# Seven half-size products for the output matmul, and other runs for the strided heads' loads

## The chip, the cores and the metric

One NeuronCore of a Trainium2 chip. The metric is the device time of one execution in microseconds (us). TensorE multiplies and writes PSUM; VectorE and ScalarE read PSUM and work element by element; GpSimd (POOL) works on SBUF alone; SyncE (SP) issues the transfers between HBM and SBUF in the order of its queue.

## The reference

```python
def reference(**kwargs):
    attn_out = _attn_ref(q, k, v)          # 4 batches, 8 heads, 576 tokens, 64 wide
    x = attn_out.transpose(0, 2, 1, 3).reshape(2304, 512)
    x = _moe_ref(x, w_in, w_out, g_ln)     # 512 -> 1024 -> h*softmax(h), normalised -> 512
    a, b = x @ w_a, x @ w_b                # 512 -> 1536
    return (a * b @ w_out2).astype(np.float32)   # 1536 -> 512
```

Heads 0 to 3 attend to the last 32 tokens, heads 4 to 7 to the tokens whose distance is a multiple of 32. The weights are float64.

## The kernel before, in words

Products are made from 16-bit halves: each operand is split into a high part (ScalarE) and a remainder (VectorE), and a product is three matmul passes, high-high, high-low and low-high (`PASSES`).

The first stage runs attention batch by batch. A group is two heads. `load_qk` loads q and k of a group, for strided heads as runs of two tokens (512 bytes) on 96 partitions; `group_T` transposes them on TensorE, six transposes of 96 columns, and ScalarE evicts them into an order by residue (L661). The tiles of batch 0 (`direct`) write their scaled probabilities into a zeroed buffer `pfb` that holds one of the two `lnT` buffers. `moe1` and `s2` are the first two dense layers and follow the batches; their results go to HBM as `y_scr`.

The second stage is three passes (`ps`) over three blocks of 768 tokens (`n`). Pass `ps` covers two of six weight columns (`u`). For a block and a `u`, `ab` calls `product` twice, for x @ w_a and x @ w_b. `product` already uses seven half-size products in place of eight (14 tiles of 6 matmuls of 384 columns a `u`, L1332): operands are A11 to S4 of the weights, from `split_ab`, and B11 to T4 of y, from `y_load`, and the partial sums are carried from bank to bank by ScalarE copies (L1339). `ab` multiplies the two results (L1381) and splits the product into `p` (L1382, L1384). `out_tile` then multiplies `p` of both `u` with the output weights `wo`, 12 matmuls of 512 columns a tile of 128 tokens (L1397), six tiles a block. In pass one ScalarE scales the result (L1407); in passes two and three VectorE adds it to the partial sums of the pass before (L1404), loaded from `o_scr` into `op`. A block's six tiles come right behind its two `ab`.

`y_load` brings a block of y into `yst` (one buffer, L1221), normalises it and makes its seven operands (L1279, L1284). `conv_ab` and `conv_o` convert the weights of the next pass beside the products; `conv_o` stages in the `wo` buffer itself, of which there are two. The weights of a and b have four buffers by `u`.

PSUM in the second stage: five banks `M` for the products, two `o` for the output, one `Q` for small things. Buffers come from rings; the user of a ring's slot waits for all users of the slot's last buffer, and no buffer is started before the one ahead of it in its ring.

The order of the work is a planner's (`Plan.schedule`): every operation has a cost and a key, a list scheduler orders each engine by key, and 200 passes with noise from a seeded generator look for the order with the shortest modelled time. The emitted program keeps that order on each engine.

Of the kernel before, what the change touches and what calls it, by code (L numbers as in the profile page):

```python
# [10 lines left out]
F32 = mybir.dt.float32  # L11
# [22 lines left out]
NM = S // QT  # L34
QB = 64
# [19 lines left out]
PARAM = dict(back=12, first=40, early=(0,), seed=6, noise=0.1, direct=(0,), stay=0.0, pf1=(),  # L55
             pf2=(), ph1=(), pv=(), pp=(8,), ps1=(), ps2=(), ps3=False, ps4=False, passes=200, e=3,
# [272 lines left out]
def tile_banded_attention_solu_bilinear(  # L329
# [86 lines left out]
    rsqs = const.tile([128, NTT], F32, name="rsqs")  # L416
    zmo = const.tile([128, NP, NCH // NP + 1], F32, name="zmo")
# [4 lines left out]

    for tag, shape, dt in (("rawq", [QT, NM, 2, D], F32), ("rawk", [QT, NM, 2, D], F32)):
        ring("at", tag, shape, dt, pm["raw"])
# [6 lines left out]
    ring("at", "e", [128, 4 * KB], F32, pm["e"])  # L431
# [9 lines left out]
    ring("conv", "sq2", [128, 512], BF16, 2)  # L441
# [36 lines left out]
    def constants_d():  # L478
        nc.gpsimd.memset(mone, -1.0)
        nc.gpsimd.memset(ones_sq, 1.0)  # L480
        nc.gpsimd.memset(onesb, 1.0)
        nc.gpsimd.memset(units, 1.0)
        nc.gpsimd.memset(units[:, 0, 1:2], 1.0 / PSCALE)
        nc.gpsimd.memset(units[:, 1, 1:2], 1.0 / LSCALE)
# [7 lines left out]
    if pm["direct"]:  # L492
# [7 lines left out]
    def from_f64(src, cols, dst=None, dtok=(), fr="f64f", need=(), ps=False):  # L500
# [11 lines left out]
        else:  # L512
            dve(0.5, lambda: nc.vector.tensor_scalar(raw()[:, :, 0], raw()[:, :, 0], 29, None,
                                                     op0=ALU.logical_shift_right), (), (raw,))
        g = f if dst is None else dst if callable(dst) else lambda: dst
# [24 lines left out]
    def load_wout(c):  # L540
        fo = wout_f32(c)
        f = from_f64(w_out[128 * c:128 * c + 128, :], False, fo, (("wof", c),), ps=c in pm["ps2"])
        act(0.9, lambda: nc.scalar.activation(f(), fo, AF.Abs, scale=g_sb[:, c:c + 1], accum_out=wam[:, c:c + 1]),
            ("g", ("wof", c)), (f, ("wam", c)))

    def pow2_scale(am, toks, n, unit, dst, dtok, top=14, least=60, ps="scp", sm=""):


        tp = rings[ps].new()
# [46 lines left out]

    def load_qk(g):
        h0 = 2 * g.pr
        g.raw = [rings[t].new() for t in ("rawq", "rawk")]
        for c, src in ((0, q), (1, k)):  # L600
            t = g.raw[c]
            if g.strided:
                dma(lambda t=t, src=src: nc.sync.dma_start(
                    out=t().rearrange("p i j d -> p i (j d)"),
                    in_=src[g.b, h0:h0 + 2].rearrange("h (i p j) d -> p (h i) (j d)", p=QT, j=2)),
                    (), ((t, 0), (t, 1)), 294912)
                continue
            for h in range(2):
                dma(lambda t=t, h=h, src=src: nc.sync.dma_start(
                    out=t()[:, :, h], in_=src[g.b, h0 + h].rearrange("(m p) d -> p m d", p=QT)),  # L610
# [33 lines left out]
    def group_T(g):  # L644
        g.T = rings["qkT"].new()
        for c in range(2):
# [3 lines left out]
            def transposes(tp=tp, raw=raw):  # L650
                for m in range(NM):
                    i, o = divmod(m, NM // 2)
                    nc.tensor.transpose(tp()[:, i, QT * o:QT * o + QT], raw()[:, m].rearrange("p h d -> p (h d)"),  # L653
                                        ident[:QT, :QT])
            pe(NM * 0.085, transposes, ((raw, 0), (raw, 1), "ident"), (tp,), NM * 144)

            def evac(c=c, tp=tp):
                src = tp()[:, :, :S // 2]
                dst, sc = g.T()[:, c], 1.0 if c else D ** -0.5
                if g.strided:  # L660
                    nc.scalar.activation(dst.rearrange("p (h a t) -> p h a t", h=2, t=NR),  # L661
                                         src.rearrange("p h (t a) -> p h a t", t=NR), AF.Copy, scale=sc)
                else:
                    nc.scalar.activation(dst.rearrange("p (i t) -> p i t", i=2), src, AF.Copy, scale=sc)
            act(1.2 if g.strided else 0.66, evac, (tp,), ((g.T, c),))
# [33 lines left out]

    def att_tile(g, j, fine):  # L700
# [3 lines left out]
        direct = g.b in pm["direct"]  # L704
# [48 lines left out]
        el = ng * nk * 1.25e-3  # L753

        def ev():
            return e()[:, :ng * nk].rearrange("p (c k) -> p c k", c=ng)
# [11 lines left out]
        else:  # L768
            dve(0.07 + el, lambda: nc.vector.tensor_tensor(
                ev().rearrange("p (f c) k -> p f c k", c=npb), sv(),  # L770
                mv().unsqueeze(3).to_broadcast([128, len(banks), npb, nk]), op=ALU.add), (*spt, mx), (e,))
# [5 lines left out]
        dve(0.08, lambda: nc.vector.tensor_scalar(s4()[:, :ng], s4()[:, :ng], u, 1e-9 * u, op0=ALU.mult, op1=ALU.add), (), ss)  # L777
# [5 lines left out]
        if direct:  # L783
            early = g.b in pm["early"]
            pt = rings["y"].new() if early else sp
            tok = (pfb, i % 4)

            def pf():
                return pfb().rearrange("p a f t -> p (a f t)").bitcast(F32)[:, 512 * (i % 4):512 * (i % 4) + ng * W]

            def blocks(t):
# [705 lines left out]
```

## Time and profile before

| | us |
|---|---|
| median of 3 timed runs (lowest to highest) | 712.41 (712.12 to 713.53) |
| the profiled execution | 714.81 |
| its span, first to last instruction | 712.7 |
| TensorE, VectorE, ScalarE, GpSimd busy | 684.6, 494.1, 404.1, 150.5 |

The profile belongs to one execution. Busy time is given by engine, by stretch of the span, and by groups of instructions (line, engine, operation, output and input). The chain that ended last follows the end of the program back to what released each step. "Clock" is the TensorE clock that was granted, as a share of full speed. Overlapping instructions of one engine are counted once in a stretch, and with their whole length in a group's mean.

### The profile page before, as it was taken

What the parts mean: (1) busy time and instruction counts of PE and PEld (TensorE: products, weight loads), DVE (VectorE), ACT (ScalarE), POOL (GpSimd) and SP (SyncE); (2) the same over time, 40 slices, a digit from 0 to 9 for tenths busy, and PEclk for the clock granted to TensorE, in tenths of its full rate; (3) what the DMA queues carried; (4) which work ended last, traced back from release to release, by engine and by line L of the source; (5) the groups of instructions that cost most, each with busy time, mean ns of one, the idle gap of its engine ahead of it and who ended that gap; (6) DMA issues with size and microseconds to landing.
All of it is one profiled execution on the core that took longest, in us unless ns stands there. A gap on an engine that the chain in (4) does not pass through costs nothing.

```text
span 712.7 us, 14218 instructions
## 1 busy us (share of the span) xinstructions
PE 684.6 (96%) x5492; PEld 452.6 (64%) x5492; DVE 494.1 (69%) x1011; ACT 404.1 (57%) x766; POOL 150.5 (21%) x266
## 2 busy tenths in 40 slices
PE   6886899999999999989999999999999999999997
PEld 5674687887887888866555555555555555465553
DVE  5889888677889747987999986656477534434352
ACT  3778677777788646856777585633354423132230
POOL 4554437544656722310000000000000000000000
PEclk9967699999999999999999999999999999999999
DMA  9988979999999946567363253345205043602304
GB/s 182 239 227 206 181 160 186 227 202 221 218 197 246 218 95 169 127 201 255 121 230 101 80 173 132 104 142 179 87 30 178 1 148 88 226 20 77 101 15 162
DMA packets 159327, 109.61 MB, mean 154 GB/s; under 512 B 103702, under 2 KB 137500, under 8 KB 159260
## 3 DMA queue, kind: packets, MB, share of 16 engines
q1 hardware_dynamic: 159260, 108.71, 59.1%
q8 instruction: 43, 0.70, 0.4%
q14 instruction: 24, 0.20, 0.1%
HBM read 65.42 MB, written 27.53 MB: 130 GB/s over the span
## 4 chain that ended last, share of the span: by engine, by line
PE 80%; DVE 6%; DMA 6%; ACT 2%; POOL 2%; issue 2%; SPq 0%; DVEq 0%; ACTq 0%; POOLq 0%
PE M L1332 33%; PE o L1397 19%; PE h L901 12%; PE y L955 11%; DMA raw<-in_moe_w_in_dram 3%; PE s L653 1%; DMA lnT<-ln 1%; PE s L744 1%; DMA PT<-P 1%; PE xbank L848 1%; DMA rawk<-in_k_dram 1%; POOL P L830 1%; DVE wk L916 1%; DVE st L906 1%; DVE y L1279 1%
## 5 line engine op out<-in xcount | busy, mean ns | idle before, releaser
L1332 PE MATMUL M<-y,w 128*128 128x384 f16 x1512 | 255.6, 326 | 0.1
L1332 PEld LDWEIGHTS <-w 128*128 128x128 f16 x1512 | 147.8, 98 | 100.9 <-issue 0.5
L1397 PE MATMUL o<-wo,p 128*128 128x512 f16 x648 | 147.4, 379 | 0.0
L1397 PEld LDWEIGHTS <-p 128*128 128x128 f16 x648 | 63.3, 98 | 71.3
L955 PE MATMUL y<-lnT,wout 128*128 128x256 f16 x864 | 102.5, 276 | 3.5 <-DMA lnT<-ln 3.4
L955 PEld LDWEIGHTS <-wout 128*128 128x128 f16 x864 | 83.2, 99 | 17.6 <-issue 6.6
L901 PE MATMUL h<-win,xh 128*128 128x512 f32 x288 | 81.5, 424 | 1.9 <-DVE wk L916 1.9
L1339 ACT COPY M<-M 128x384 f32<-128x384 f32 x72 | 33.5, 466 | 64.4 <-PE M L1332 64.3
L901 PEld LDWEIGHTS h<-win,xh 128*128 128x128 f32 x288 | 55.5, 201 | 14.3 <-DVE wk L916 1.4
L1404 DVE SCALAR_TENSOR_TENSOR ob<-o,osc,op 128x512 f32<-128x512 f32 x36 | 27.0, 751 | 44.3 <-PE o L1397 43.3
L1382 ACT ACTIVATE p<-A 128x384 f16<-128x384 f32 x72 | 36.8, 521 | 31.5 <-DVE A L1381 31.4
L1384 DVE SCALAR_TENSOR_TENSOR p<-A,p 128x384 f16<-128x384 f32 x72 | 39.0, 553 | 11.1 <-ACT p L1382 10.8
L1381 DVE TENSOR_TENSOR A<-A,M 128x384 f32<-128x384 f32 x36 | 19.9, 553 | 37.6 <-PE M L1332 37.4
L507 ACT ACTIVATE f64f<-raw 128x512 f32<-128x512 f32 x52 | 34.7, 673 | 14.3 <-DMA raw<-in_moe_w_in_dram 6.1
L1343 DVE TENSOR_TENSOR A<-M,V 128x384 f32<-128x384 f32 x36 | 19.9, 555 | 32.2 <-PE M L1332 32.2
L1354 ACT COPY V<-M 128x384 f32<-128x384 f32 x36 | 17.1, 475 | 43.0 <-PE M L1332 42.9
L901 PE MATMUL h<-win,xl 128*128 128x512 f32 x144 | 40.8, 406 | 0.0
L830 POOL TENSOR_TENSOR P<-e,P 128x324 f16<-128x324 f32 (+2 forms) x30 | 32.0, 1072 | 14.5 <-ACT P L829 14.4
L822 POOL TENSOR_TENSOR e<-e,r 128x324 f32<-128x324 f32 (+2 forms) x30 | 26.9, 902 | 33.1 <-DVE r L778 24.2
L901 PEld LDWEIGHTS h<-win,xl 128*128 128x128 f32 x144 | 26.9, 193 | 5.6
L906 DVE TENSOR_REDUCE st<-h 128x1 f32<-128x1024 f32 x18 | 21.9, 1218 | 11.0 <-PE h L901 10.9
L916 DVE SCALAR_TENSOR_TENSOR wk<-h,st,wk 128x1024 f32<-128x1024 f32 x18 | 23.1, 1281 | 9.2 <-POOL st L914 7.4
(173 smaller groups left out, 1051.0 us busy)
## 6 DMA issues: line engine op xcount, KB each, us to landing
raw<-in_moe_w_out_dram SPq DMA_DIRECT2D x20, 512.0 KB
o_scr<-ob SPq DMA_DIRECT2D x36, 256.0 KB
op<-o_scr SPq DMA_DIRECT2D x36, 256.0 KB
raw<-in_moe_w_a_dram SPq DMA_DIRECT2D x12, 512.0 KB
raw<-in_moe_w_b_dram SPq DMA_DIRECT2D x12, 512.0 KB
y_scr<-y SPq DMA_DIRECT2D x14, 384.0 KB
y<-y_scr SPq DMA_DIRECT2D x14, 384.0 KB
y_scr<-ys SPq DMA_DIRECT2D x18, 256.0 KB
```

The costliest lines, as they stand in the source:

```text
L507: act(0.67, lambda: nc.scalar.activation(f(), raw()[:, :, 1].bitcast(F32), AF.Prelu, scale=2.0 ** -112, alpha=-2.0 ** 32), (raw,), (f,))
L830: pool(0.15 + 1.4 * pl, lambda: nc.gpsimd.tensor_tensor(plo, ev(), ph, op=ALU.subtract), (e, ("P2", pi, 0)), (("P2", pi, 1),))
L901: nc.tensor.matmul(h()[:, 512 * n:512 * n + 512], xs[xa]()[:, kk], win[wa][:, kk, 512 * n:512 * n + 512], start=(pi == 0 and kk == 0), sto ...
L906: dve(1.22, lambda: nc.vector.tensor_reduce(st()[:, 0:1], h(), axis=AX.X, op=ALU.max, negate=True), (h,), ((st, 0),))
L916: dve(1.21, lambda: nc.vector.scalar_tensor_tensor(e(), h(), st()[:, 7:8], e(), op0=ALU.mult, op1=ALU.mult, accum_out=st()[:, 2:3]), (h, ( ...
L955: nc.tensor.matmul(y()[:, 256 * mi:256 * mi + 256], wout[:, kk, wa, 128 * m:128 * m + 128], lnT()[:, xa, kk], start=(pi == 0 and kk == 0), ...
L1332: nc.tensor.matmul(bank()[:, :HB], w()[:, wa, a, kk], y7[b]()[:, xa, kk], start=first and pi == 0 and kk == 0, stop=pi == 2 and kk == 1, s ...
L1339: act(TA, lambda: nc.scalar.copy(dst()[:, :HB], src()[:, :HB]), (src,), (dst,))
L1382: act(TA, lambda x=x, v=v: nc.scalar.activation(v(0), x(), AF.Copy, scale=2.0 ** -PEXP), (x,), ((pu, 0, c, t),))
L1384: dve(TD, lambda x=x, v=v: nc.vector.scalar_tensor_tensor(v(1), x(), 2.0 ** -PEXP, v(0), op0=ALU.mult, op1=ALU.subtract), (x, (pu, 0, c, t ...
L1397: nc.tensor.matmul(o(), pus[u]()[:, xa, c, 128 * tt:128 * tt + 128], wo()[:, 2 * u + c, wa], start=(u == 0 and c == 0 and pi == 0), stop=( ...
L1404: dve(0.75, lambda: nc.vector.scalar_tensor_tensor(ob(), o(), osc()[:, tt:tt + 1], op(), op0=ALU.mult, op1=ALU.add), (o, osc, op), (ob,))
```

## The change

The output product of passes two and three (`so=(1, 2)`) is done by `out_pair` for two tiles of 128 tokens at once, as seven products of half the contraction and half the columns (256), on sums of `p` that `ab` makes on VectorE and sums of the output weights that `split_o` makes. Pass one keeps `out_tile`. A block's output product is issued after the first `ab` of the next block (in the last block after the second). PSUM becomes four banks `M` and four `N`, each a ring of its own. The weights of a and b have three buffers instead of four, `wo` one instead of two; `conv_o` stages in `yst`. The old partial sums are loaded into the buffer the result is stored from. Strided q and k are loaded as runs of eight tokens on 72 partitions and transposed eight times by 72 columns; the tiles of batch 0 write their probabilities in place, in three zeroed `e` buffers; the squares of the conversions go into the raw buffer. The planner's seed and several costs change. The core of the diff:

```diff
-PARAM = dict(back=12, first=40, early=(0,), seed=6, noise=0.1, direct=(0,), stay=0.0, pf1=(),
+PARAM = dict(back=12, first=40, early=(0,), seed=4, noise=0.1, direct=((0, 0), (0, 1)), stay=0.0, pf1=(),
...
-        pfb = rings["lnT"].new()
-        dve(2.0, lambda: nc.vector.memset(pfb(), 0.0), (), [(pfb, k) for k in range(4)])
+    for i, t in enumerate(e_t):
+        dve(0.3, lambda t=t: nc.vector.memset(t, 0.0), (), (("e0", i),))
...
-                    in_=src[g.b, h0:h0 + 2].rearrange("h (i p j) d -> p (h i) (j d)", p=QT, j=2)),
-                    (), ((t, 0), (t, 1)), 294912)
+                    out=pairs(t), in_=src[g.b, h0:h0 + 2].rearrange("h (p i) d -> p h (i d)", p=QS)),
+                    (), ((t, 0), (t, 1)), 210000)
...
-                for m in range(NM):
+                n = QS if g.strided else QT
+                for m in range(S // n):
...
-    for i in range(4):
+    for i in range(3):
         for m in range(2):
             ring("w2c" if i > 1 else "w2a", f"w{m}{i}", [128, 2, 7, 2, 128], F16, 1, c_c if i > 1 else c_a)
...
-    ring("ps2a", "M", [128, 512], F32, 5, c_a)
+    for tag, early in (("M", 3), ("N", 2)):
+        for i in range(4):
+            ring("ps2a" if i < early else "ps2b", f"{tag}{i}", [128, 512], F32, 1, c_a if i < early else c_c)
...
-    ring("w2c", "wo", [128, NCH // NP + 1, 2, DM], F16, 2, c_c)
-    ring("w2c", "ob", [128, DM], F32, 2, c_c)
-    ring("w2c", "op", [128, DM], F32, 2, c_c)
-    ring("ps2b", "o", [128, DM], F32, 2, c_c)
-    ring("ps2b", "Q", [128, 512], F32, 1, c_c)
+    ring("w2c", "wo", [128, UP, 7, 2, DM // 2], F16, 1, c_c)
+    ring("w2c", "ob", [128, 2, DM], F32, 2, c_c)
...
     def conv_o(ps):
-        wo = WO[ps] = rings["wo"].new()
+        st = rings["yst"].new()
...
+            def sums(T=T, c0=c0):
+                f, g = f32(c0), f32(c0 + 1)
+                t = T().rearrange("p (s n) -> p s n", s=4)
+                b11, b12, b21, b22 = f[:, :256], f[:, 256:], g[:, :256], g[:, 256:]
+                for k_, (x, y) in enumerate(((b12, b11), (b22, t[:, 0]), (b22, b12), (b21, t[:, 1]))):
+                    (nc.gpsimd if pm["osum"] else nc.vector).tensor_tensor(t[:, k_], x, y, op=ALU.subtract)
...
+            if (t, c) == (1, 0):
+                s1, s2 = rings["A"].new(), rings["A"].new()
+                summed(s1, x[1, 0], x[1, 1], ALU.add)
+                half(pu, S1, s1)
+                summed(s2, s1, x[0, 0], ALU.subtract)
+                half(pu, S2, s2)
+                summed(x[1, 0], x[0, 0], x[1, 0], ALU.subtract)
+                half(pu, S3, x[1, 0])
+        if halves:
+            summed(x[0, 1], x[0, 1], s2, ALU.subtract)
+            half(pu, S4, x[0, 1])
...
+    def out_pair(ps, n, pus, tt, osc, cut):
+        Y, X, ob = bank("M"), bank("N"), rings["ob"].new()
...
+            def mm():
+                for u in range(UP):
+                    for pi, (xa, wa) in enumerate(PASSES):
+                        nc.tensor.matmul(bk(i), pus[u](xa, a)[:, 128 * tt:128 * tt + 128], wo()[:, u, b, wa],
+                                         start=a == A11 and u == 0 and pi == 0, stop=u == UP - 1 and pi == 2,
+                                         skip_group_check=a != A11)
...
+        mult(1, A11, B11)
+        mult(4, S1, T1)
+        again(1, 2)
+        mult(2, S2, T2)
+        mult(1, A12, B21)
+        again(2, 3)
+        mult(3, S3, T3)
+        mult(2, S4, B22)
+        add(3, 1, 1, ps)
+        add(2, 0, 1, ps)
+        mult(3, A22, T4)
+        add(4, 1, 1, 1)
+        add(4, 0, 1, 1)
+        add(1, 0, 0, ps)
+        add(3, 1, 0, ps)
...
+        for u in range(UP):
+            P.key = at(b0) + u * TU
+            last = b0 == NP * NSB - 1
+            pus.append(ab(Y7[n], UP * ps + u, last and u == UP - 1))
+            if u != (UP - 1 if last else 0):
+                continue
+            if before:
+                out_block(*before)
+                if ps and not i:
+                    P.key = at(b0) - 20
+                    split_o(ps)
+            if ps < NP - 1 and i == NSB - 1:
+                P.key = at(b0) - 20
+                conv_ab(UP * (ps + 1) + 1)
+        before = ps, n, pus, b0
...
+    out_block(*before)
```

Here `again` is a ScalarE copy between halves of the banks X and Y, and `add` a VectorE addition of a half bank into `ob`, scaled.

## Rows read from the trace of the kernel before

**Rows 1.** The page, part 1: busy time, share of the span, instructions.
```profile
PE 684.6 (96%) x5492; PEld 452.6 (64%) x5492; DVE 494.1 (69%) x1011; ACT 404.1 (57%) x766; POOL 150.5 (21%) x266
```

**Rows 2.** Windows: stretch, length; busy PE, PEld, DVE, ACT, POOL; clock, DMA share, GB/s.
```profile
0.00:20.00 20.00, 13.75 (x171) 10.85 (x172) 12.01 (x32) 7.72 (x14) 9.92 (x30) 1.00 1.06 187
...
140.00:180.00 40.00, 40.00 (x513) 32.12 (x511) 31.48 (x58) 30.74 (x55) 16.70 (x31) 1.00 0.99 217
...
340.00:380.00 40.00, 39.88 (x228) 22.16 (x227) 37.35 (x79) 29.91 (x59) 0.00 (x0) 1.00 0.56 188
380.00:420.00 40.00, 40.00 (x221) 21.39 (x219) 36.30 (x69) 26.87 (x49) 0.00 (x0) 1.00 0.30 98
420.00:460.00 40.00, 40.00 (x227) 22.07 (x226) 27.21 (x65) 26.22 (x54) 0.00 (x0) 1.00 0.41 134
460.00:500.00 40.00, 40.00 (x228) 22.04 (x226) 23.16 (x46) 15.27 (x33) 0.00 (x0) 1.00 0.48 152
500.00:540.00 40.00, 40.00 (x230) 22.32 (x229) 24.21 (x54) 17.64 (x36) 0.00 (x0) 1.00 0.24 78
540.00:580.00 40.00, 40.00 (x222) 21.51 (x221) 22.85 (x47) 15.07 (x32) 0.00 (x0) 1.00 0.28 87
...
660.00:700.00 40.00, 40.00 (x227) 22.07 (x226) 16.26 (x29) 10.76 (x23) 0.00 (x0) 1.00 0.20 67
700.00:712.70 12.70, 8.73 (x41) 3.76 (x39) 3.00 (x4) 0.00 (x0) 0.00 (x0) 0.98 0.51 165
```

**Rows 3.** The chain that ended last, pieces on PE: start, length, line, matmuls.
```profile
244.97 5.25 PE y L955 x48
...
581.85 19.50 PE M L1332 x120
...
693.20 15.55 PE o L1397 x72
```

**Rows 4.** Groups by line and form: weight loads, VectorE and ScalarE prices.
```profile
L1397 PEld LDWEIGHTS <-p 128*128 128x128 f16 x648 | 63.3, 98 | 71.3
...
L1384 DVE SCALAR_TENSOR_TENSOR p<-A,p 128x384 f16<-128x384 f32 x72 | 39.0, 553 | 11.1 <-ACT p L1382 10.8
...
L1404 DVE SCALAR_TENSOR_TENSOR ob<-o,osc,op 128x512 f32<-128x512 f32 x36 | 27.0, 751 | 44.3 <-PE o L1397 43.3 <-DMA op<-o_scr 0.8
...
L1170 DVE SCALAR_TENSOR_TENSOR w<-f64f,small,w 128x256 f16<-128x256 f32 x12 | 5.7, 479 | 0.0
```

**Rows 5.** Timeline of VectorE around the handover: start, length, line.
```profile
318.14 0.95 DVE L1279 SCALAR_TENSOR_TENSOR y<-yst,y 128x768 f16<-128x768 f32 x1
...
331.38 1.02 DVE L1381 TENSOR_TENSOR A<-A,C 128x384 f32<-128x384 f32 x2
...
358.61 0.95 DVE L1284 TENSOR_TENSOR yst<-yst 128x768 f32<-128x768 f32 x1
```

**Rows 6.** Timeline of SP's queue and then of PE, same stretch.
```profile
321.73 0.55 SPq L1221 DMA_DIRECT2D yst<-y_scr  x1
...
343.85 1.46 PE L1397 MATMUL o<-wo,p 128*128 128x512 f16 x6
...
347.41 9.31 PE L1332 MATMUL M<-y,w 128*128 128x384 f16 x54
...
366.28 2.75 PE L1397 MATMUL o<-wo,p 128*128 128x512 f16 x12
```

**Rows 7.** Timeline of the last microseconds, VectorE.
```profile
708.77 0.75 DVE L1404 SCALAR_TENSOR_TENSOR ob<-o,osc,op 128x512 f32<-128x512 f32 x1 [1.84 <-PE o L1397]
```

**Rows 8.** Groups by line and form, and one stretch of the first microseconds.
```profile
L653 PE MATMUL s<-ident,rawq 96*128 96x96 f32 x96 | 14.4, 300 | 7.2 <-DMA rawq<-in_q_dram 4.6 <-issue 2.6
...
L661 ACT ACTIVATE qkT<-s 128x576 f32<-128x576 f32 x16 | 10.3, 648 | 8.5 <-PE s L653 8.4
L664 ACT ACTIVATE qkT<-s 128x576 f32<-128x576 f32 x16 | 10.1, 645 | 4.1 <-PE s L653 4.1
...
2.90:3.90 1.00, 0.00 (x0) 0.00 (x0) 0.97 (x1) 0.00 (x0) 0.87 (x3) 1.00 1.20 271
```

More of the change, by code (lines that the diff above doesn't have):

```diff
@@ L34 @@
 NM = S // QT
+QS = 72
 QB = 64
@@ L1141, in conv_ab @@
             if u >= UP:
-                scale_ab(u, m, rings["Q"].new())
+                scale_ab(u, m, bank("M"))
             split_ab(u, m, fs)
@@ L1232, in y_load @@
         for h in range(2):
-            tp, R = misc.new(), rings["R"].new()
+            tp, R = bank("M"), rings["R"].new()
             Rs.append(R)
@@ L1323, in product, with mult @@
     def product(y7, u, m):
-        b1, b4, b2, b3 = [rings["M"].new() for _ in range(4)]
+        b1, b4, b2, b3 = [bank(x) for x in "MMNN"]
         w = WU[u, m]
-        def mult(bank, a, b, first):
+        def mult(to, a, b, first):
             def mm():
@@ new lines, in ab @@
+    def ab(y7, u, spare=False):
+        halves = u // UP in pm["so"]
+        a, b = product(y7, u, 0), product(y7, u, 1)
+        if spare:
+            pu = Halves(*(rings[f"w{m}{NU % 3}"].new() for m in range(2)))
+        else:
+            pu = Halves(rings[f"p{count_p[0] % 3}"].new())
+            count_p[0] += 1
+        x = {}
+        for (x_, c, t), (y, _, _) in zip(a, b):
+            x[t, c] = x_
+            dve(TD, lambda x=x_, y=y: nc.vector.scalar_tensor_tensor(x(), x(), 2.0 ** -PEXP, y()[:, :HB], op0=ALU.mult,
+                                                                     op1=ALU.mult), (y,), (x_,))
+            if not halves:
+                half(pu, 2 * t + c, x_)
+                continue
+            if (t, c) != (1, 0):
+                half(pu, {(0, 0): A11, (0, 1): A12, (1, 1): A22}[t, c], x_)
+            if (t, c) == (1, 0):
[9 more added lines that the diff above has]
+            half(pu, S4, x[0, 1])
+        return pu
@@ L1418, in tile_banded_attention_solu_bilinear @@
     P.key = at(0) + pm["cv"]
-    prime()
+    for i in range(4):
+        P.key = at(0) + pm["cv"] + (20.0 if i > 1 else 0.0)
+        prime(i)
+    P.key = at(0) + pm["cv"]
     for u in range(UP):
@@ new lines, in out_block @@
+    def out_block(ps, n, pus, b0):
+        osc = rings["osc"].new()
+        P.key = at(b0) + UP * TU - 3
+        dve(0.2, lambda: nc.vector.tensor_scalar(osc(), YSC[n](), ksc[:, ps, 1:2], None, op0=ALU.mult),
+            (YSC[n], ("ksc", ps)), (osc,))
+        for tt in range(SB // 256):
+            P.key = at(b0) + UP * TU + tt * TO
+            if ps in pm["so"]:
+                out_pair(ps, n, pus, tt, osc, b0 == NP * NSB - 1 and tt == SB // 256 - 1)
+            else:
+                ob = rings["ob"].new()
+                for k in range(2):
+                    out_tile(ps, n, pus, 2 * tt + k, osc, ob, k)
@@ new lines, in tile_banded_attention_solu_bilinear @@
+    before = None
+    for b0 in range(NP * NSB):
+        ps, i = divmod(b0, NSB)
+        n = (i + ps) % NSB
+        if b0:
+            P.key = at(b0) - 30
+            if not ps:
+                y_load(n)
+            elif i == NSB - 1:
+                y_reload(n)
+        pus = []
+        for u in range(UP):
[3 more added lines that the diff above has]
+            if u != (UP - 1 if last else 0):
+                continue
+            if before:
[7 more added lines that the diff above has]
+        before = ps, n, pus, b0
+        P.key = at(b0) + 10
+        if ps < NP - 1 and not i:
+            conv_ab(UP * (ps + 1))
+        if ps < NP - 1 and i == NSB - 1:
+            conv_o(ps + 1)
```

327 lines of the change are left out of this document (193 added, 134 removed).

## The prediction

> **What bounds the kernel now.** I read the page's shares first: TensorE is busy 96% of the span, VectorE 69%, ScalarE 57% [rows 1]. A share is a mean over stages, so the windows table came next [rows 2]. It shows two regimes. In the first 20 us TensorE has work for 13.75 of 20 us while the DMA share is over 1.0: the start waits for data. From 140 us on it is busy 40.00 of every 40 us or just under, at clock 1.00, up to the last stretch, where it ends some 4 us ahead of the span. From there to the end the kernel takes as long as its matmuls take, and only two things can change that: fewer TensorE cycles, or a gap that opens in them. The chain that ended last confirms it: its late pieces are TensorE alone, and a piece with its number of matmuls gives the pace [rows 3]. 120 matmuls of 384 columns (L1332) take 19.50 us, 162.5 ns each; 72 of 512 columns (L1397) take 15.55 us, 216.0 ns; 48 of 256 columns (L955) take 5.25 us, 109.4 ns. From 256 to 512 columns that is 106.6 ns for 256 columns, so 0.416 ns a column and 2.8 ns a matmul, with a new weight load before each.
>
> **The output product, removed and added.** Before, two 128-token tiles take 2 x 12 matmuls of 512 columns: 24 x 216.0 = 5.18 us. After, the pair takes 7 products x 2 u x 3 passes = 42 matmuls of 256 columns: 42 x 109.4 = 4.59 us. That is 0.59 us a pair, and passes two and three have 2 x 3 blocks x 3 pairs = 18 pairs: 18 x 0.587 = **10.6 us** less on the engine that sets the end. Pass one keeps its 512-column form. Weight loads rise from 24 to 42 a pair, at 98 ns busy each [rows 4]; the 109.4 ns pace of L955 already holds such a load per matmul.
>
> The Trainium skill, page "TensorE: Matmul & The Clock Gate", section "Back-to-back issue gap", speaks against this: it gives a sustained 81 ns for 128 columns and 131 ns for 512. By it 256 columns would take some 98 ns (my estimate, between its two), a pair 42 x 98 = 4.1 us against 24 x 131 = 3.1 us, and the change would cost 17 us. The paces of [rows 3] contradict it by 85 ns at 512 columns.
>
> **VectorE.** Each of the 12 half-width blocks of passes two and three gains four sums and three remainders of 384 elements, 7 x 0.553 = 3.9 us, 46 us together. A pair now ends in six half-width adds instead of two of 512: no row shows 256 elements read from PSUM, so I take 0.479 (the 256-wide form of L1170) and bound it by 0.751 above [rows 4]: 6 x 0.479 - 2 x 0.751 = 1.4 us a pair, 25 us together. The sums of the output weights add some 5 us in each of two passes. All of it lies beside TensorE. Passes two and three use VectorE for 23 of each 40 us at 460 to 580 and 16 of 40 near the end; some 119 us in 240, which with these 81 makes 200 of some 230. That such a load can be hidden is seen at 340 to 420: VectorE 37.35 and 36.30 of 40, TensorE 39.88 and 40.00 [rows 2]. I cost it at nothing; without cover it is the second rival. ScalarE gains three half-precision copies a block and two bank copies a pair; it has 15 to 18 of 40 there and is left out.
>
> **The order of the output product.** A block's output product is now issued behind the first `ab` of the next block, and since every product draws its banks from the rings M0 to M3 and N0 to N3 in program order, it can't be pulled ahead. In passes two and three this gives VectorE a whole product (84 matmuls, 13.65 us) to prepare the sums, and I take no stall there. At the start of pass one it takes a cover away. There the second block's y is being prepared: its first transfer into `yst` is issued at 321.73, and its last difference runs at 358.61 [rows 5, 6]. Meanwhile TensorE ran output matmuls of the first block: 6 at 343.85, the last 12 at 366.28, 60 in all, 13.0 us. These can't run there any more. The second block's own first product is wanted directly behind the first block's, at about 345, and spreads over 13.65 us, so its last operand is wanted at some 357.
>
> The change also sends the four output-weight parts through `yst` (one buffer), between the first block's y and the second's. VectorE's last read of the first y starts at 318.14 [rows 5]; 1 MB at the 188 GB/s of that stretch [rows 2] and four splits of at most 0.75 put some 8 us in front of the second y. With 8 us for its own 1.5 MB and some 17 us of VectorE (13 operations of 0.95, four of 0.5, two roots of 1.2), its last operand is there at 318 + 1 + 8 + 8 + 17 = 352 if VectorE does nothing else, and near 363 if the first block's own 24 operations (back to back 0.47 to 0.51 each, the two of 331.38 [rows 5]) all go first. Against 357 that is a gap of 0 to 6 us, 0 to 13 as outer bounds. The planner reorders by lateness, so neither end is likely: I take **+4 us**.
>
> **The end.** The last tile's matmuls used to run in one piece of 15.55 us [rows 3], with a VectorE add of 0.75 and a store behind it [rows 7]. A pair's last product must now wait for two adds on its X bank, at least 2 x 0.479, and only the other pairs can fill that. The previous block's output product, put behind the last `ab`, covers the sums before it. Bounds 0 and 2.4 (a wait of 1.2 in two pairs); I take **+1.2**. The old partial sums are now read into the buffer that the result is stored from, two pairs of it; a read waits in SP's queue for the store two pairs back, with the later stores and weight loads behind it. At a DMA share of 0.20 to 0.48 I cost that at nothing.
>
> **The strided loads and the attention.** A strided transpose set is 8 of 72 columns instead of 6 of 96: the same columns; were it paid per instruction, two more at 0.15 (14.4 us over 96, which counts overlap) would be 0.3 us a set, bounded by zero below. Its eviction with a stride takes 648 ns against 645 without one, so a gentler stride gives nothing [rows 8]. One 288 KB load needs 1.09 us at the 271 GB/s of the first loads [rows 8]; only the eight loads of batches 0 and 1 fall where data is waited for. Bounds: a quarter off each, -2 us, or a third more, +3; I take 0. The same page family has a rule here: "DMA: Bandwidth & Descriptors" of the Trainium skill, section "Why a DMA increments its semaphore by 16 and not by 1", lets a transfer use the largest number of engines up to 16 that divides its rows, 12 for 72 rows and 16 for 96. No row shows single DMA engines; by it the +3 would be the value. The memset of the old probability buffer gives way to three smaller ones, beside the first loads: 0.
>
> **Sum.** -10.6 + 4 + 1.2 = -5.4 us. The profiled execution took 714.81 us (span 712.70), 2.4 above the median of the three timed runs; it would become 709.4, and the median 712.41 becomes **707.0**.
>
> **The rivals.**
> *The handover loses all its cover.* Pass one, between its first and second block: TensorE waits the 13.0 us of output matmuls it no longer has. -10.6 + 13.0 + 1.2 = +3.6: 716.0, slower. It decides from a gap of 9.4 us on. For it: one `yst` buffer for three users, VectorE nearly full there. Against: half of what VectorE does there can wait.
> *VectorE becomes the bound in pass two.* 460 to 580 holds 70.2 us of VectorE [rows 2]; added are 6 x 3.9 + 9 x 1.4 + 5 = 41, 111 of the 115 us that TensorE then needs, and the third weight buffer (four before) pushes a conversion from pass one towards it. If 5 to 6 us stick out: -10.6 + 4 + 1.2 + 5.5 = 0.1, 712.5, no change. Against: two adjacent operations overlap (331.38: 1.02 for two of 0.553).
> *The whole gain arrives.* The planner closes both gaps and the longer runs spare 2 us at the start: -12.6, 699.8.
> *A price per matmul rather than per column,* in every output pair. It decides from 5.18 / 42 = 123 ns on; at the 162.5 ns of the 384-column form a pair takes 6.83 us, 18 x 1.64 = +30, 747. The 109.4 of L955 [rows 3] excludes nearly all of it. By the page named above it would be 735.
> *The load part does nothing* of what its description says: it is inside the forecast, since I cost it at 0.
>
> **How the numbers follow.** Forecast 0.57 (its own range 702 to 711), the whole gain 0.16, VectorE bound 0.13, handover lost 0.12, price per matmul 0.02. A measurement here tells 0.2%, 1.4 us, from no change. Faster: 0.57 + 0.16 and a fifth of the VectorE case, 0.76. Same: most of the rest of it, 0.10. Slower: 0.14. The range reaches from the whole gain to nearly the lost handover, 700 to 715, and leaves out the tail of that one and the last rival.
>
> **What would show it.** The output matmuls of passes two and three at 109 ns with 256 columns, 756 of them beside 216 of 512, and TensorE's last matmul earlier by the sum. A TensorE gap between 340 and 365 that ends on VectorE's y splits, 4 us or so. VectorE at 33 to 37 of 40 in pass two with TensorE at 40.00 beside it. The start unchanged within 3 us. It is wrong if TensorE shows gaps of several microseconds in passes two and three, or if the second half starts earlier or later by more than 3 us.

## The result and the profile after

The changed kernel took **705.92 us** in the median (704.70 to 706.70) beside 712.97 us (712.12 to 715.01) for the kernel before: a ratio of **0.9895** with a 95% interval of 0.9869 to 0.9922. The forecast was 707.0, faster. The size came out; two of the reasons did not, as the runs below show: the end loses time to a wait that was costed at nothing, and part of the whole gain belongs to the planner's seed, which the prediction does not mention at all. (Each run has its own executions of the kernel before beside it; a ratio is near that of the means, and so not quite the quotient of two medians.)

In the changed kernel the products stand in L1392 (before L1332), whole output tiles in L1499 (L1397), the output product by halves in L1530 with its additions in L1546 (L1404), remainders of `p` in L1489 (L1384), the first stage's gate projection in L912 (L901) and its second projection in L966 (L955).

The page, part 1, and the windows table, which answer to [rows 1] and [rows 2]; the last row of the windows is the stretch that serves as a ruler below, from the start of the last matmul of `h` (L912) to the end of the last matmul of all:

```profile
PE 671.1 (95%) x5861; PEld 483.9 (69%) x5861; DVE 557.6 (79%) x1189; ACT 429.2 (61%) x842; POOL 145.2 (21%) x268
```

```profile
340.00:380.00 40.00, 38.13 (x212) 20.51 (x210) 37.32 (x80) 27.91 (x50) 0.00 (x0) 1.00 0.45 155
...
460.00:500.00 40.00, 40.00 (x278) 26.92 (x275) 35.83 (x81) 25.81 (x51) 0.00 (x0) 1.00 0.45 143
500.00:540.00 40.00, 40.00 (x290) 28.09 (x288) 34.79 (x80) 18.43 (x46) 0.00 (x0) 1.00 0.39 130
...
580.00:620.00 40.00, 40.00 (x289) 28.21 (x290) 34.42 (x76) 19.49 (x42) 0.00 (x0) 1.00 0.48 155
...
660.00:700.00 40.00, 36.85 (x308) 29.86 (x306) 25.24 (x57) 10.70 (x26) 0.00 (x0) 1.00 0.34 114
...
290.70:700.66 409.96, 404.94 (x2743) 267.35 (x2742) 333.66 (x719) 229.79 (x470) 5.98 (x10) 1.00 0.39 127
```

VectorE rose from 23 to 35 of 40 us in pass two and TensorE kept its 40.00 beside it. Two stretches are short: 340 to 380 by 1.9 us and 660 to 700 by 3.1. The waits of TensorE from 300 us on name both, and the chain that ended last shows the pace and the end:

```profile
PE N L1530 <- DVE ob L1546: 3.1, 2, 1.7
PE M L1392 <- DVE y L1335: 0.9, 2, 0.5
PE M L1499 <- DVE A L1459: 0.6, 1, 0.6
PE M L1499 <- ACT A L1420: 0.4, 1, 0.4
```

```profile
667.63 1.97 PE N L1530 x18
...
691.20 0.49 DVE ob L1546
...
691.71 3.06 DMA out_dram<-ob
...
694.84 3.44 DMA ob<-o_scr
...
698.39 2.44 DVE ob L1546 x6
```

18 matmuls of 256 columns in 1.97 us are 109 ns each, the forecast's price. The end hangs on no matmul: an addition frees an `ob` buffer, its store takes 3.06 us, only then is the next pair's old sum read into it (3.44 us), and the additions that free TensorE's banks wait for that.

The same ruler in the kernel before, its windows row and its one wait there; the first row is the stretch in which the wait lies:

```profile
300.00:340.00 40.00, 37.63 (x265) 26.46 (x263) 33.79 (x73) 26.51 (x50) 4.02 (x4) 0.96 0.64 207
...
290.40:708.75 418.35, 415.73 (x2403) 235.62 (x2401) 265.52 (x536) 198.14 (x390) 8.35 (x11) 1.00 0.39 124
```

```profile
PE y L955 <- DMA lnT<-ln: 2.4, 1, 2.4
```

So the stretch went from 418.35 to 409.96 us, 8.4 less: TensorE's busy time from 415.73 to 404.94, its gaps from 2.6 to 5.0. What lies ahead of it went from 290.4 to 290.7, what lies behind the last matmul from 3.95 to 3.54. That adds up to the 8.5 us between the two spans (712.7 and 704.2). The ruler is the tool of what follows: it holds nearly the same matmuls, how long the first stage took doesn't enter it, and two traces of the kernel before put it at 418.35 and 418.25. A new order can still move a little work across its start; where that happens, it is counted below.

### The profile page after: what moved, and what is told of

Read it like the earlier page. It is cut to its first block, busy times and chain, and to the rows that moved or that the text cites. A ratio compares the mean times of both kernels' runs of the same rounds, so it can differ in the third digit from the quotient of the medians.

```text
span 704.2 us, 15205 instructions
## 1 busy us (share of the span) xinstructions
PE 671.1 (95%) x5861; PEld 483.9 (69%) x5861; DVE 557.6 (79%) x1189; ACT 429.2 (61%) x842; POOL 145.2 (21%) x268
## 4 chain that ended last, share of the span: by engine, by line
PE 85%; DVE 5%; DMA 4%; ACT 2%; issue 1%; SPq 1%; POOL 0%; DVEq 0%; POOLq 0%; ACTq 0%
PE N L1392 19%; PE M L1392 14%; PE h L912 13%; PE y L966 13%; PE M L1499 6%; PE N L1530 6%; PE M L1530 5%; PE s L664 2%; DMA raw<-in_moe_w_a_dram 1%; PE s L757 1%; PE xbank L859 1%; DMA raw<-in_moe_w_b_dram 1%; DMA rawq<-in_q_dram 1%; DMA raw<-in_moe_w_in_dram 1%; DVE f64f L520 1%
## 5 line engine op out<-in xcount | busy, mean ns | idle before, releaser
L1392 PEld LDWEIGHTS <-w 128*128 128x128 f16 x1512 | 147.9, 98 | 95.3 <-issue 1.3
L1392 PE MATMUL N<-y,w 128*128 128x384 f16 x864 | 155.5, 326 | 0.0
L1392 PE MATMUL M<-y,w 128*128 128x384 f16 x648 | 119.2, 326 | 0.9 <-DVE y L1335 0.9
L966 PE MATMUL y<-lnT,wout 128*128 128x256 f16 x864 | 102.8, 275 | 2.1 <-ACT wout L579 2.1
L966 PEld LDWEIGHTS <-wout 128*128 128x128 f16 x864 | 82.5, 98 | 15.3 <-ACT wout L579 2.4
L912 PE MATMUL h<-win,xh 128*128 128x512 f32 x288 | 80.7, 423 | 2.4 <-DVE wk L927 2.4
L1530 PEld LDWEIGHTS <-p 128*128 128x128 f16 x693 | 67.7, 98 | 15.6 <-issue 3.5
L912 PEld LDWEIGHTS h<-win,xh 128*128 128x128 f32 x288 | 55.8, 201 | 14.5 <-DVE wk L927 2.6
L1484 ACT CAST p<-A 128x384 f16<-128x384 f32 x101 | 50.5, 512 | 22.1 <-DVE A L1459 19.6
L1489 DVE TENSOR_TENSOR p<-A,p 128x384 f16<-128x384 f32 x101 | 54.6, 552 | 6.6 <-ACT p L1484 6.4
L1530 PE MATMUL N<-wo,p 128*128 128x256 f16 x396 | 51.4, 273 | 3.1 <-DVE ob L1546 3.1
L1499 PE MATMUL M<-wo,p 128*128 128x512 f16 x216 | 49.9, 379 | 1.0 <-DVE A L1459 0.6
L912 PE MATMUL h<-win,xl 128*128 128x512 f32 x144 | 40.1, 401 | 0.0
L1530 PE MATMUL M<-wo,p 128*128 128x256 f16 x297 | 38.6, 273 | 0.0
L1499 PEld LDWEIGHTS <-p 128*128 128x128 f16 x216 | 21.1, 98 | 24.6 <-issue 1.5
L1546 DVE SCALAR_TENSOR_TENSOR ob<-N,osc,ob 128x256 f32<-128x256 f32 x54 | 24.3, 477 | 14.3 <-PE N L1530 10.1
L1399 ACT COPY N<-N 128x384 f32<-128x384 f32 x36 | 16.6, 465 | 30.1 <-PE N L1392 29.5
L912 PEld LDWEIGHTS h<-win,xl 128*128 128x128 f32 x144 | 27.4, 194 | 6.4 <-issue 0.2
```

The lines of the kernel that those rows point to most:

```text
L912: nc.tensor.matmul(h()[:, 512 * n:512 * n + 512], xs[xa]()[:, kk], win[wa][:, kk, 512 * n:512 * n + 512], start=(pi == 0 and kk == 0), sto ...
L966: nc.tensor.matmul(y()[:, 256 * mi:256 * mi + 256], wout[:, kk, wa, 128 * m:128 * m + 128], lnT()[:, xa, kk], start=(pi == 0 and kk == 0), ...
L1392: nc.tensor.matmul(to()[:, :HB], w()[:, wa, a, kk], y7[b]()[:, xa, kk], start=first and pi == 0 and kk == 0, stop=pi == 2 and kk == 1, ski ...
L1484: act(0.5, lambda: nc.scalar.copy(pu(0, a), x()), (x,), (pu.tok(0, a),))
L1489: dve(TD, lambda: nc.vector.tensor_tensor(pu(1, a), x(), pu(0, a), op=ALU.subtract), (x, pu.tok(0, a)), (pu.tok(1, a),))
L1499: nc.tensor.matmul(o(), pus[u](xa, 2 * t + c)[:, 128 * w:128 * w + 128], wo_whole(ps, 2 * u + c)[:, wa], start=(u == 0 and c == 0 and pi = ...
```

## The experiments

### Whole tiles, and halves in one pass: what the columns are worth

```diff
-so=(1, 2)
+so=()        # first kernel
+so=(1,)      # second kernel
```

> All three passes make the output product from whole tiles (512 columns), everything else as in the changed kernel; the planner orders anew. My theory: the seven products are the gain, and they cost a tail. 10.6 us of columns come back, the 3.1 us of TensorE gaps at the end go: 705.9 + 10.6 - 3.1 = 713.4 us. Rival (the new order, the banks and the loads carry the gain): 706 us, within 2. Between them, near 710: both have a share.

> Only pass two makes its output product by halves, pass three makes whole tiles as before (a new plan with it). Over the same stretch (383.6 us in the changed kernel, 388.6 in the kernel before): theory (each pass by halves takes 5.3 us of TensorE columns, and the wait for old sums at the end, 3.1 us, belongs to the halves of pass three alone): 383.6 + 5.3 - 3.1 = 385.8 us, and TensorE has no gap over 1 us behind its last product. Rival (the gain came with the new plan and not with the columns): 383.6 or less.

The planner makes a new order for each list of operations. The ruler's rows of the two kernels:

```profile
300.50:719.10 418.60, 414.38 (x2408) 235.02 (x2406) 257.40 (x521) 193.42 (x382) 6.29 (x10) 1.00 0.37 124
```

```profile
293.20:706.43 413.23, 409.47 (x2570) 250.85 (x2568) 293.92 (x618) 210.74 (x424) 6.33 (x11) 1.00 0.38 126
```

No pass by halves 418.60 us, one 413.23, two 409.96, or 407.43 without the wait at the end (below). TensorE's busy time falls by 4.9 us a pass (414.38, 409.47, and 404.60 without that wait), where the forecast had 5.3. By the measure of the second expectation (last matmul of L966, 321.5, to the last of all, 706.43) one pass by halves takes 384.9 us beside the forecast 385.8, and there is no gap over 1 us behind the last product, since the wait at the end belongs to halves in pass three. So the columns pay.

The whole times are another matter: 721.69 us, a ratio of 1.0152 (1.0118 to 1.0186), for whole tiles, and 712.16, 1.0007 (0.9982 to 1.0031), for halves in one pass. The first was expected at 713.4, and missed by 8 us (by the ratio, 10). The rows say where: its last matmul of `h` starts at 300.5 instead of 290.4. The profiled execution, 725.09 us, was 3.4 above its median, so the new order cost the first stage some 7 to 10 us, about as much as what was being measured, or more. From here on both numbers are given, the start of the ruler and its length.

### The old loads of the strided heads

```diff
-                    out=pairs(t), in_=src[g.b, h0:h0 + 2].rearrange("h (p i) d -> p h (i d)", p=QS)),
+                    ... in_=src[g.b, h0:h0 + 2].rearrange("h (i p j) d -> p (h i) (j d)", p=QT, j=2)),
```

(with the transposes by 96 columns that belong to it; in the traces VectorE, ScalarE, GpSimd and SyncE run the changed kernel's order from start to end)

> Strided q and k loaded as before (runs of two tokens on 96 partitions, six transposes of 96 columns, the old eviction order), the order of all instructions kept. My theory: the loads are worth nothing, 705.9 within 1.4 us. Rival one (longer runs spare time at the start): about 2 us slower, 708, the gap in the first 100 us. Rival two (72 partitions use fewer DMA engines): up to 3 us faster, 703.

703.62 us, 0.9892 (0.9859 to 0.9924), beside 0.9895 for the whole change; ruler 409.08, from 287.4. The runs of eight tokens are worth nothing that shows, the forecast's value, though either interval is some 2 us wide to each side. The prediction quoted the Trainium skill, page "DMA: Bandwidth & Descriptors", section "Why a DMA increments its semaphore by 16 and not by 1": 12 engines for 72 rows against 16 for 96. The prediction's +3 us for that would make this run 0.9853, just outside its interval; a smaller effect is not excluded, and whether 12 engines ran no row here shows.

### A third buffer for the old sums

```diff
-    ring("w2c", "ob", [128, 2, DM], F32, 2, c_c)
+    ring("w2c", "ob", [128, 2, DM], F32, 3, c_c)
```

> Three output buffers instead of two. My theory: the end hangs on the read of old partial sums into a buffer whose store (3.06 us on the chain) has to land first, with 3.44 us for the read; with a third buffer the last pair's read starts earlier and the 3.1 us of TensorE gaps at the end shrink to under 1: 705.9 - 2.5 = 703.4 us. Rival (the gaps come from the two adds on bank X that a pair's last product waits for): 705.9 within 1 us, the gaps stay.

700.07 us, 0.9860 (0.9825 to 0.9894), where the expectation comes to 0.9866. Ruler and the wait at the end:

```profile
287.40:694.83 407.43, 404.60 (x2743) 267.46 (x2741) 333.47 (x719) 230.57 (x469) 5.95 (x10) 1.00 0.39 129
```

```profile
PE N L1530 <- DVE ob L1546: 1.0, 1, 1.0
```

Two gaps, 3.1 us together, became one of 1.0: the read of old sums no longer waits for a store. 2.1 us of the end were that wait, and the 1.0 left is the one that the forecast did have (two additions on bank X, 1.2). The ruler is 407.43 beside 409.08 in the kernel above, which ran on the same chip with two buffers, and 409.96 in the changed kernel. The whole time gained more than these 2 us, but its order of the first stage is a new one too (start 287.4); the kernel with the remainders on GpSimd, below, has three buffers and the changed kernel's own first stage, and is the cleaner witness.

### How much of VectorE is hidden

The remainders of S2, S3 and S4 are computed n times by VectorE, the order kept:

```diff
-            dve(TD, lambda: nc.vector.tensor_tensor(pu(1, a), x(), pu(0, a), op=ALU.subtract),
+            def rest(n=2 if a > 3 else 1):          # n=4 in the second kernel
+                for _ in range(n):
+                    nc.vector.tensor_tensor(pu(1, a), x(), pu(0, a), op=ALU.subtract)
```

> The fp16 remainders of the four combined operands S2, S3, S4 (and their fellows) of passes two and three are computed twice by VectorE, in the same order of work: 36 more instructions of about 0.55 us, some 18 us of VectorE in the two passes. Theory (VectorE is covered: TensorE is busy all 40 us of each slice from 380 to 660 us while VectorE is busy 28 to 36 of 40, about 55 us idle in all): within 2 us of the changed kernel's ratio of 0.9895 to the kernel before, that is 0.989 to 0.993. Rival (VectorE stands on the path to each out product, so that its own time counts): slower by most of the 18 us, a ratio of 1.01 or more.

> The same remainders are computed four times: 108 more VectorE instructions, some 50 to 60 us in passes two and three. Theory (throughput of VectorE decides where its cover ends): the 55 idle us from 380 to 660 us are used up, and in the heavy stretch from 460 to 620 us, where 20 us are idle, VectorE becomes the bound: 10 to 35 us slower than the changed kernel, a ratio of 1.00 to 1.04, with TensorE gaps that end on VectorE's adds or on the remainders. Rival one (TensorE has enough ready work whatever VectorE does): no slower than twice computed. Rival two (each remainder is on the path): slower by all of the 55 us, a ratio of 1.065.

Twice: 704.36 us, 0.9909 (0.9876 to 0.9943). VectorE's busy time in the ruler rose by 17.5 us, TensorE's wall time by 0.6:

```profile
291.40:701.97 410.57, 406.04 (x2743) 267.80 (x2741) 351.17 (x755) 230.14 (x469) 6.00 (x10) 1.00 0.39 127
...
500.00:540.00 40.00, 40.00 (x291) 28.17 (x290) 37.52 (x83) 19.45 (x47) 0.00 (x0) 1.00 0.39 130
```

At 37.5 of 40 us VectorE still stands beside a TensorE at 40.00. Four times: 745.63 us, 1.0487 (1.0454 to 1.0520). The ruler, the two waits that lead the list and two rows of TensorE's timeline:

```profile
288.30:740.55 452.25, 420.36 (x2743) 270.49 (x2742) 390.31 (x827) 229.64 (x470) 5.99 (x10) 0.97 0.35 115
```

```profile
PE N L1532 <- DVE p L1491: 10.8, 10, 2.4
PE N L1392 <- DVE A L1403: 4.3, 2, 2.3
```

```profile
658.00 1.14 PE L1392 MATMUL M<-y,w 128*128 128x384 f16 x6
661.18 2.02 PE L1392 MATMUL N<-y,w 128*128 128x384 f16 x6 [2.04 <-DVE A L1403]
```

56.7 us more of VectorE cost 42.3 us: past the bound, as the theory said, and further past it than its 10 to 35, between that and the second rival's 55. Part of the excess is in the second timeline row: behind a gap of 2.04 us the same six matmuls take 2.02 us instead of 1.14, at a granted clock of 0.53 from 661.2 to 662.4, next to the lower of its two levels (1.2 GHz), where it was 1.00 ahead of the gap. The 2743 matmuls were busy for 420.4 us instead of 404.9, so gaps of 31.9 us instead of 5.0 cost another 15.4. So the cover in passes two and three ends somewhere between 18 and 57 us beyond what the change uses, and the rival of a VectorE bound in pass two, which needed 5 us to stick out, did not come near: from 460 to 580 us VectorE was busy for 105.5 of 120.

### The remainders of the sums on GpSimd

```diff
-plo2=()
+plo2=(4, 5, 6)      # and three ob buffers
```

> Three buffers for old sums as in the run above, and the 36 remainders of the combined operands of passes two and three are made on GpSimd, which has nothing to do after 340 us, instead of on VectorE (about 1.1 us each by GpSimd's own nearest rows, for 0.55 us on VectorE). Stretch from the last matmul of the gate projection (the line of h) to the last matmul of all: 418.4 us in the kernel before, 410.0 in the changed kernel, 407.4 with three buffers. Theory (VectorE is covered in passes two and three, so relieving it buys nothing there): 407 to 408.5. Rival (VectorE's 20 us matter at the handover and at the end): 404 to 406. Second rival (GpSimd's slower remainders come late for TensorE): over 410.

702.24 us, 0.9869 (0.9838 to 0.9899), with a ruler of 407.47 from 291.4, next to 407.43 with three buffers alone: relieving VectorE buys nothing, the first theory. Against the changed kernel, whose order of the first stage it shares, the 2.5 us of the ruler are the third buffer's.

### Pass one by halves too

```diff
-so=(1, 2)
+so=(0, 1, 2)        # first kernel; with plo2=(4, 5, 6) and three ob buffers in the second
```

> Pass one too makes its output product by halves (a new plan of the order of work with it). Measured over the stretch that the change touches, from the last matmul of the first stage to the last matmul of all (383.6 us in the changed kernel): theory (in pass one VectorE is busy 36 to 37 of 40 us already, so the 5.3 us of TensorE columns that go are paid with waits for VectorE): between 2 us shorter and 5 us longer. Rival (the cover holds there too): 5 us shorter, 378.5.

> All three passes by halves, three buffers for old sums, and the 54 remainders of the combined operands on GpSimd. With all passes by halves and the remainders on VectorE the same stretch was 421.9 us, 5.3 of them by 48 matmuls of the first stage that this plan leaves for later. Theory (what was lost there is VectorE's time in the handover, where it was busy 39.4 of 40 us): relieved by 10 us in pass one it gives the columns of pass one too, 407.4 - 5.3 = 402 us, up to 405, net of work of the first stage left for later. Rival (the remainders of the combined operands are not what holds VectorE at the handover): 414 or more. Second rival (late remainders of GpSimd): gaps of TensorE that end on GpSimd.

722.37 us, 1.0161 (1.0129 to 1.0194), and 709.85, 0.9978 (0.9952 to 1.0005). The rows of the first, then of the second:

```profile
293.70:715.64 421.94, 409.69 (x2942) 288.35 (x2940) 359.09 (x782) 247.36 (x526) 13.21 (x11) 0.98 0.38 123
...
340.00:380.00 40.00, 30.14 (x161) 16.34 (x160) 39.40 (x74) 27.45 (x48) 0.00 (x0) 0.83 0.34 116
```

```profile
288.50:702.38 413.88, 406.52 (x2936) 287.28 (x2934) 351.44 (x726) 247.49 (x523) 71.96 (x65) 0.99 0.38 126
...
340.00:380.00 40.00, 34.27 (x220) 21.94 (x218) 39.36 (x74) 29.68 (x58) 4.54 (x4) 0.91 0.45 155
```

The measure named in the first expectation gives 380.3 and misleads: this order runs 48 matmuls of L966 late, among the products, so the mark itself moved from 317 to 335. By the ruler, less those 48 (5.25 us at 109.4 ns), it is 416.7 against 410.0: the columns of pass one (4.9) went, and some 12 us came. That is more than the theory allowed and the opposite of the rival. The place is the handover, from the first block of pass one to the second: VectorE at 39.4 of 40, TensorE at 30.1, the largest wait 3.8 us on VectorE's additions of a product (L1403). Of the 12 us 7.2 are gaps; the rest is slower matmuls, the granted clock being 0.83 over that row, and 0.50 from 355.3 to 356.5, the lower of its two levels (1.2 GHz), behind gaps of 3.85 and 1.26 us.

In the second kernel, with 54 remainders taken off VectorE, three buffers, and 40 late matmuls subtracted (4.4 us), the ruler is 409.5, where 407.4 - 4.9 = 402.5 was to be had. The 12 us lost became 7, and the handover is still where they are lost, with VectorE still at 39.4. No gap of TensorE ends on GpSimd; the largest wait is now on ScalarE's squares of the second block's y (L1295). The two largest waits, first kernel, then second:

```profile
PE N L1392 <- DVE A L1403: 3.8, 1, 3.8
...
PE M L1300 <- ACT Z L1295: 2.6, 3, 1.8
```

The result lies between the two theories, and both left out `yst`. That one buffer takes the output weights first and the second block's y after VectorE's last read of them; with pass one by halves VectorE also makes the sums of the weights from it. The last read and the load of y, in the changed kernel, the first and the second:

```profile
327.24 0.74 DVE L1234 SCALAR_TENSOR_TENSOR wo<-yst,small,wo 128x512 f16<-128x512 f32 x1
328.01 1.22 SPq L1277 DMA_DIRECT2D yst<-y_scr  x2
...
343.71 1.80 DVE L1267 SCALAR_TENSOR_TENSOR wo<-yst,small,wo 128x512 f16<-128x512 f32 x3
345.54 1.21 SPq L1277 DMA_DIRECT2D yst<-y_scr  x2
...
339.44 0.74 DVE L1267 SCALAR_TENSOR_TENSOR wo<-yst,small,wo 128x512 f16<-128x512 f32 x1
340.21 1.22 SPq L1277 DMA_DIRECT2D yst<-y_scr  x2
```

Counted from the start of the ruler, y is loaded 37.3 us in, and 51.8 and 51.7 in the two kernels: the 54 remainders on GpSimd didn't bring it forward. So the remainders are at most a part of what is lost there; a second `yst` buffer wasn't tried. Pass one is rightly left whole as the kernel stands.

### The seed

The change also moves the planner's seed from 6 to 4.

```diff
-early=(0,), seed=4,
+early=(0,), seed=6,       # the changed kernel with the old seed
```

> Only the planner's seed, 6 as before instead of 4. It says how much of any difference between two plans is chance. My theory: within 2 us of 705.9, since TensorE is full in both. Rival (the seed carries a good part of the gain): 709 or more.

```diff
-early=(0,), seed=6,
+early=(0,), seed=4,       # the kernel before with the new seed
```

> The kernel before with the planner's seed 6 in place of 4, nothing else. Theory (the seed shuffles the first stage alone, by some us either way): the stretch from the last matmul of the gate projection to the last matmul of all stays at 416 to 419 us, and the ratio to the kernel before moves only by what the first stage gains or loses, 0.99 to 1.015. Rival (the plan matters in the stretch of the change as much): the stretch differs by more than 3 us.

> The kernel before with the planner's seed 4, which the change brings with it, in place of its own seed 6, and nothing else. (The run above that was called by seed 6 is, seed 6 being the kernel's own, the kernel before itself.) The changed kernel with seed 6 gained only 0.34%, with seed 4 1.05%, with the same stretch behind the last matmul of the gate projection (410.4 and 410.0 us). Theory (a seed is good or bad for one list of operations, and says nothing of the change): the stretch stays at 418 to 419 us, and the ratio comes out between 0.995 and 1.02, decided by the first stage (start of the last matmul of the gate projection, 288 to 290 us in the kernel before). Rival (seed 4 is a better order for either kernel, worth 4 us by itself): a ratio of 0.993 or less, with that start at 286 or before. Further: the wait for lnT of 2.3 us at 303 us, there in two profiles of the kernel before, goes or stays with the seed.

The middle one's edit was empty, because seed 6 was the kernel's own: that run is the kernel before again, and its ratio of 1.0007 (0.9981 to 1.0033) is that of no change at all. Its ruler is 418.25, from 288.2, with the wait for `lnT` at 2.3 us.

The changed kernel with seed 6 took 707.44 us, 0.9966 (0.9938 to 0.9995). The kernel **before** with seed 4 took 707.21 us, **0.9923** (0.9894 to 0.9953): the rival, not the theory. The first one's executions spread from 705.03 to 712.93; its median would be within the 2 us of its theory, its ratio is the rival's (0.9966 of 712.97 is 710.5). Their rulers:

```profile
292.00:702.40 410.40, 405.26 (x2743) 267.51 (x2741) 333.64 (x720) 230.55 (x469) 9.05 (x11) 1.00 0.40 129
```

```profile
283.80:700.28 416.48, 414.35 (x2403) 234.77 (x2401) 262.97 (x533) 196.06 (x386) 5.94 (x11) 1.00 0.38 125
```

With seed 4 the old kernel's first stage is through at 283.8 instead of 288.2 to 290.4, and the wait for `lnT` shrinks to 1.4 us. The seed by itself is worth 0.77%, the change without it 0.34%; together 1.11%, beside the 1.05% measured for both. With either seed the change itself is worth some 0.3%, and the interval of each ratio is about as wide to each side.

What the starts of the ruler leave open: with seed 4 the old list of operations is through its first stage at 283.8, the new one at 288.3 to 291.4 (four traces of the changed kernel's order of that stage); with seed 6 at 288.2 to 290.4 and at 292.0. A part of the spread is that of executions: the two traces of the kernel before differ by 2.2 us in the span and in this start alike. Taking off each profiled execution's distance from its kernel's median (an estimate), the new list is some 4 to 6 us later there under either seed, and that is most of what the 6.5 to 8 us gained in the ruler lose again. Whether one of the first stage's edits does it (the tiles of batch 0 written in place, the zeroed buffers), or only how the draw fell, wasn't tried. The loads aren't quite out of it: with the old ones in the same order the start is 287.4, or 289 by the same estimate, beside 288.2 to 290.6 with the new ones.

## Why the prediction was right, and where it was wrong

- **The columns, -10.6.** Right. 109 ns a matmul of 256 columns, as read from L955; the busy time fell by 4.9 us a pass, 9.8 together, and the ruler by 5.4 from none to one pass by halves. The busy time of the change itself fell by 10.8, because the kernel before also ran L955 slowly behind its gap (its 192 matmuls in the ruler took 23.8 us, in the changed kernel 22.0, with the granted clock of that stretch at 0.96 and 1.00). The sustained 131 ns for 512 columns that the prediction quoted from the Trainium skill, page "TensorE: Matmul & The Clock Gate", section "Back-to-back issue gap", would have made this +17: the runs exclude it.
- **The handover, +4.** The right place, and half the size: 1.9 us. 0.9 of it is on the releaser that was named, the y splits (L1335); the other 1.0 are output tiles (L1499) that wait for a PSUM bank `M` which VectorE (L1459) or ScalarE (L1420) still reads. The chain through `yst` was seen rightly: the second y, put some 8 us later, was loaded at 328.01 instead of 321.73. With all passes by halves it is loaded 14 us later still, VectorE fills the stretch, and 12 us are lost.
- **The end, +1.2, with the read of old sums at nothing.** The second half of this step failed. "A read waits in SP's queue for the store two pairs back ... I cost that at nothing" was sized by the DMA share of 0.20 to 0.48. A share says nothing of a chain: one store of 3.06 us and one read of 3.44, in series, 6.5 us together, stood in the way, while a pair's matmuls take 4.6. The gaps were 3.1 us; a third buffer takes them to 1.0, close to the 1.2 for the two additions alone.
- **VectorE, 0.** Right. 68 us more in the ruler, estimated at 81, covered but for the wait at the end; a further 17.5 cost 0.6.
- **The strided loads, 0.** Right as far as it shows: 0.9892 without them, 0.9895 with them.
- **The start, "unchanged within 3 us".** True of the two traces (290.4 and 290.7; 288.2 in the other trace of the kernel before), and luck. It is a sum of two things that the prediction did not price: the seed, which stood in the diff and takes 4 to 7 us off the old kernel's first stage, and a later first stage of the new list.
- **TensorE full "from 140 us on".** Not quite: in the kernel before it was busy for 37.63 of 40 us from 300 to 340, at a granted clock of 0.96. The wait of 2.4 us for `lnT` at 303 us went with the change and stood in no term.

Summed from the profiles: -9.8 for columns, -1 for L955's slower matmuls and -2.4 for the gap at 303, +1.9 at the handover, +3.1 at the end make -8.2 of the ruler's -8.4; with +0.3 ahead of it and -0.4 behind it that is the 8.5 between the spans, and 7.0 between the medians (the profiled execution of the kernel before was 1.8 above its median). The forecast's -5.4 had two errors that nearly cancel (2.1 too much at the handover, 1.9 too little at the end); the gap at 303 and the slower matmuls behind it make the rest. The rival in which the whole gain arrives, at 699.8 (a ratio of 0.982), wasn't reached even with three buffers: their 700.07 us is a ratio of 0.9860, and the handover still waits.

## What to carry to other kernels

Where a planner with a random seed orders the program, a change of the seed is an edit like any other: here the old kernel gained 0.77% from it alone, more than the changed kernel gained without it, and a new list of operations moved the first stage by some 7 to 10 us in one case. Measure such a change with a ruler that begins behind the part that is reshuffled, and try the old kernel with the new seed before crediting the change. When a buffer is stored from and loaded into, price the store and the load as a chain against the interval at which the buffer is wanted, whatever the DMA share is; and when one buffer serves several uses in turn, as `yst` here, price the last read of the one before the load of the next. The best kernel here is the change with three `ob` buffers, 700.07 us; the old kernel's early first stage together with it wasn't tried.

## What the runs showed of the hardware

- VectorE slows while GpSimd works, and only for one kind of operation. With the remainders on GpSimd, from 380 us on (groups by line and form, that kernel):

```profile
L1489 DVE TENSOR_TENSOR p<-A,p 128x384 f16<-128x384 f32 x57 | 34.1, 605 | 2.0 <-ACT p L1484 1.7
L1481 DVE TENSOR_TENSOR A<-A 128x384 f32<-128x384 f32 x48 | 28.4, 603 | 0.3
...
L1403 DVE TENSOR_TENSOR C<-N,V 128x384 f32<-128x384 f32 x30 | 16.5, 555 | 16.5 <-PE N L1392 14.0 <-ACT V L1414 2.3
```

  In the changed kernel the three lines take 552, 551 and 554 ns. The first two read both operands from SBUF, the third reads one of its two from PSUM. The Trainium skill, page "SBUF — State Buffer", section "SBUF: two separate sides", has the rule: an operation of VectorE with two SBUF inputs and one of GpSimd take turns on a shared port pair. The trace agrees: beside 36 GpSimd operations of 0.9 to 1.8 us the 105 of VectorE's took some 5.5 us more together, and the lengthened ones are those that overlap a GpSimd operation in time (up to 1.28 us; none of the others over 0.56).
- The granted clock of the whole span varied between executions of one and the same kernel. The kernel before took 707.7 us in the median where that clock was 0.985 or more (706.2 to 710.2) and 712.6 where it was lower (707.9 to 715.7). In its two traces the difference lies between 20 and 100 us, where TensorE has gaps: 0.82, 0.76 and 0.78 in the stretches 20 to 40, 40 to 60 and 60 to 100 us in the one, 0.94, 0.84 and 0.85 in the other. With seed 4 no execution of it was below 0.983, and the six of eight at 0.985 or more took 706.4 in the median; with its own seed seven of 69 were that high. So most of what the seed gives goes with the clock of the first 100 us; which of the two brings the other was not separated.
